# Attention and gated FFN in one kernel: the third batch's first queries and keys move ahead of the last weights in the load list, and three hand-kept orders of work are replaced

## The chip, the core and the metric

The kernel runs on one core of a Trainium2 chip. The metric is the device time of one execution in microseconds (us). The core has TensorE (PE: matmuls, with PEld for its weight loads), VectorE (DVE), ScalarE (ACT), GpSimd (POOL) and SyncE (SP). POOL issues all loads from memory, SP issues the DMA transposes and most stores, ACT a few stores at the end.

## What is computed

The reference, cut to its core:

```python
# q, k, v: (8 batches, 12 heads, 448 positions, 64)
scores = scale * np.matmul(q, k.transpose(0, 1, 3, 2))
attn = np.maximum(scores, 0.0) ** 2 / S
attn_out = np.matmul(attn, v)
x = attn_out.transpose(0, 2, 1, 3).reshape(B * S, H * D)   # (3584, 768)
g = x @ w_gate                                             # (768, 1536)
out = (0.5 * g * (1.0 + erf(g / sqrt(2))) * (x @ w_val)) @ w_out
```

Attention with a squared relu in the place of softmax, and on its result a feed-forward block with a gelu gate. Inputs and output are float32; the kernel casts to bf16 while loading.

## The kernel before

**Work on TensorE.** The array is used as four quarters of 64 x 64; two row halves run as two streams of instructions, PE0 and PE1, and every matmul goes through the helper `mm` (line 400, its call of the matmul is line 401, where nearly all of PE's rows stand). Per batch there are:

- 21 score units ("s", `add_scores`): four matmuls of 64x64x448 each, then a relu on ACT (twice on DVE, in the first batch) and a square on DVE.
- 6 value products ("v", `add_values`): 14 matmuls, one for each pair of heads; their scaled result, copied by DVE or ACT, is one sixth of the batch's x (`xT`).
- gate and value sums of the FFN. A plain unit (`add_gate_value`) is 24 matmuls for one block of 128 of the 1536 columns, gate or value; batches 0 and 1 have 24 plain units each. Later batches also have units of seven products that share sums (`add_pair`, three-character names such as 2A1, 12 matmuls each).
- output products (`add_product`, names a1 to n7: 14 groups of seven products, 24 matmuls of 64x64x384 each), with weight sums made once on DVE (`add_weight_sums`, line 1139, `wt<-wo`).

A plain unit of a batch needs all six of that batch's value products, and the weights of its block: the weight tile W_i (gate half `wg`, value half `wv`) covers the blocks 2i and 2i + 1.

**Transposes of queries and keys.** A third of a batch (four heads) is called (b, m), with m from 0 to 2. For batches 0 and 1 PE transposes them ("t"). From batch 2 on, DVE regroups a third (`qkr`, line 511), and SP issues two DMA transposes of it (line 516, `add_dma_transposes`), which give `qkT`.

**The orders.** Three strings carry them.

- `START` (line 36) lists PE's first work, batch 0: transposes t00 to t21, score units s0 to s20, value products v0 to v5, single matmul pairs x0 and x1 of the first gate and value unit, and t30, batch 1's first transposes. An "a" behind a name puts that entry's copy on ACT in the place of DVE.
- `LINE` (line 12) lists all later units, 563 entries: a single digit is the next plain unit of that batch in the order of blocks, gate then value; "s" and "v" are the next score unit and value product of batches 1 to 7, "t" the next transposes of batch 1; the other names are as above, and "w0" to "w5" place weight sums on DVE.
- `LOADS` (line 33) lists the loads after batch 0's first ones. W is a gate and value weight tile, O a quarter of the output weights, "q" and "v" with a small letter are batch 0's; Qn and Vn are the queries with keys, and the values, of third n counted from batch 1: Q0 to Q2 are batch 1, Q3 and Q4 are the first two thirds of batch 2. What is in no list is loaded behind it, third by third.

**The planner.** `run_plan` (line 119) goes through these with a cost for each operation and writes each engine's program in the order of its own times. POOL's loads keep the list's order. For PE it looks at the first 12 units of `LINE` that are left (`AHEAD`, line 114; `next_unit`, line 168) and takes the first that it thinks ready, else the one that is ready soonest. The time at which it thinks a load landed comes from a sum over the loads alone:

```python
        arrivals[op] = nbytes / rate                 # load, line 432
            dma = max(dma, op.end) + arrivals[op]    # run_plan, lines 289, 290
            op.lag = dma + 2.0 - op.end
```

The programs that come out are fixed: on the chip each engine runs its own in order and waits on semaphores.

**Rings.** Queries and keys as loaded (`qk16`) have two buffers (`RING_H`), so Q_n waits for the transposes or the regrouping of the third two before it; values have three (`RING_V`), each freed by the third's last value product; `qkT` has three (`RING_T`). These waits stand on POOL's queue, in order, and hold up what is issued behind them.

**Fillers.** While PE waits in the first 24 us of the plan, `fill` puts in matmuls on a tile of zeros (`warm`, line 603).

Of the kernel before, what the change touches and what calls it, by code (L numbers as in the profile page):

```python
# [9 lines left out]


LINE = """
s s s 0 0 s t s 0 s s v 0 s s s s t s v 0 0 0 v 0 s s s s s v s v 0 s s 0 s v 0 1 0 0 1 1 1 1 s 1 0
0 1 0 s s 1 0 s s s 1 s 1 1 w1 v s s 1 1 s 0 1 1 1 0 s 1 s s 0 1 0 s s 0 1 v 1 1 1 1 a1 s a2 s s s
a7 a6 1 v a4 s a5 v s b7 s b1 s b6 v w0 a3 s s b5 b4 b2 s v 2 s b3 s 2 s 2 s 2 v 2 s 2 s s s s v s
s s v 2 s 2 2 c1 c6 v c7 s s v 2 c2 c4 2 c5 s s 2 v s s 2A1 2D1 s 2A7 2D7 w2 2A2 2A6 c3 s s s 3 2D6
2A5 2A4 v 2D2 2D4 s 3 v 2D5 2F1 s 2E1 2F2 2A3 3 s 2F6 s 2D3 2E7 2F7 s 2E6 v 2E2 2E5 2E4 2E3 3 s 2C1
2F5 s 3 2C6 2F4 2B1 2C2 v 2C7 2B6 2B7 2C5 s s s 2F3 2B5 s 2C4 s 3 2C3 w3 s s s 2B2 s 2B4 3 2B3 3 d1
d7 d6 3 3 v v s s e1 s s e2 d5 e7 d4 d3 v d2 s s s e6 v s f7 3 s 3 s f1 e4 f6 s s f5 e5 s s 4 f4 4
v s s f3 v f2 4 4 v s s e3 s s 4 4 4 s s s g7 v 4A1 s g1 s s s s v v g6 4 5 s 4A7 4A2 4A6 g5 g2 g4  # L20
4D1 4A4 s s 4E1 4A5 4E2 v s 4A3 4D7 g3 4D6 4E6 s 4D5 4D2 5 4E7 4E4 s 4B1 4E5 s s 4F1 s 4B6 v 4D4
4D3 s s 4B7 v 4B2 4G1 4B5 4B4 s 4F6 4F7 4F2 4G6 4E3 4B3 4G2 s 4H1 s 4F5 4F4 4F3 4G7 v 4C1 s s 4H2
4H7 4G5 4H6 4G4 s 4H4 4H5 s 4G3 s 4C6 s v v 4C7 4C5 4C2 5 4C4 s s 4C3 s 5 5 h7 4H3 h1 s 5 5 s h6 s
h5 i1 5 i7 s i6 s v s s s h3 v i4 h2 6B1 h4 v 6A1 s s v 6B2 i5 i3 6A6 6A2 j1 j7 j2 i2 6A7 6B7 6D1
6G1 6A4 6B6 j6 j4 6A5 6B4 w4 6D7 j5 6D6 6B5 6G6 6G7 6A3 6D2 w5 6G5 j3 6G2 6C1 6C2 6B3 6C6 6D4 6E1
6D5 6E2 6C7 6H1 6G4 6C5 6C4 6E7 6D3 6G3 6E6 6H2 6L1 6H7 6E5 6H6 6H4 6K1 6H5 6C3 6L2 6K2 6L6 6E4 6K6
6L7 6L5 6H3 6K7 6F1 6I1 6E3 6F6 6F7 6J1 6F2 6K5 6K4 6F5 6L4 6I2 6I6 6F4 6J6 6I7 6L3 6J2 6J7 6K3 6F3
6I5 6I4 6J5 k7 6J4 6I3 6J3 l1 n1 l6 k1 k6 k5 k4 k3 l7 l4 m7 m1 m2 n7 n2 m6 l5 l3 n6 m4 m5 n5 n4 l2
# [12 lines left out]

# [266 lines left out]
def kernel(  # L308
# [162 lines left out]
    def load_v(b, h0, h1, deps=()):  # L471

        m = h0 // 4
        for i in range(2):
            def emit(i=i):
                if (b, m) not in v16:
                    v16[b, m] = qkv.tile([128, 4, VC, D], bf16, name="v16", tag="v16")
                c0 = i * (SC - VC)
                return nc.gpsimd.dma_start(  # L479
                    v16[b, m][HALF[i], h0 % 4:h0 % 4 + h1 - h0, :, :],  # L480
                    v[b, h0:h1].rearrange("h (p c) d -> p h c d", c=SC)[:, :, c0:c0 + VC, :])
# [1121 lines left out]
```

## Time and profile before

| What | us |
|---|---|
| runs shown: median (lowest, highest of 3) | 394.53 (394.39, 396.39) |
| the profiled execution, first to last instruction | 397.0 |
| PE busy in it | 388.1 |
| first matmul on loaded data starts at | 5.68 |
| first score unit of batch 2 starts at | 83.22 |
| last store issued by ACT at | 392.88 |

The profiled execution is an execution of its own, 2.5 us above the median; all times of the trace below are its times, counted from its first instruction. In the rows, "x" is a count of instructions, "out<-in" names tiles, and a bracket at the end of a row gives how long the engine had been idle and what released it. Loads are counted in KB as they land (bf16), half of what is read.

### The profile page before, as it was taken

What the parts mean: (1) busy time and instruction counts of PE and PEld (TensorE: products, weight loads), DVE (VectorE), ACT (ScalarE), POOL (GpSimd) and SP (SyncE); (2) the same over time, 40 slices, a digit from 0 to 9 for tenths busy, and PEclk for the clock granted to TensorE, in tenths of its full rate; (3) what the DMA queues carried; (4) which work ended last, traced back from release to release, by engine and by line L of the source; (5) the groups of instructions that cost most, each with busy time, mean ns of one, the idle gap of its engine ahead of it and who ended that gap; (6) DMA issues with size and microseconds to landing.
All of it is one profiled execution on the core that took longest, in us unless ns stands there. A gap on an engine that the chain in (4) does not pass through costs nothing.

```text
span 397.0 us, 18156 instructions
## 1 busy us (share of the span) xinstructions
PE 388.1 (98%) x8195; PEld 335.3 (84%) x8198; DVE 297.5 (75%) x479; ACT 268.5 (68%) x428; POOL 95.7 (24%) x156
## 2 busy tenths in 40 slices
PE   7999999999999999999999999999999999999995
PEld 3355689978988998899999989889999998899994
DVE  2695795767797688889878669698999577778652
ACT  2795872266687778988577787889877656665320
POOL 5755523322233333123123333130100000000000
PEclk9999999999999999999999999999999999999999
DMA  7999999998989999856588998964302240000055
GB/s 91 168 200 198 197 207 201 93 117 105 122 152 152 199 110 179 107 73 97 71 138 144 140 200 123 146 94 56 50 2 62 64 122 2 4 3 2 23 142 160
DMA packets 76333, 44.82 MB, mean 113 GB/s; under 512 B 36832, under 2 KB 73184, under 8 KB 76256
## 3 DMA queue, kind: packets, MB, share of 16 engines
q0 software_dynamic: 37728, 24.39, 47.7%
q1 hardware_dynamic: 37888, 18.49, 26.4%
q8 instruction: 64, 1.05, 1.1%
q10 hardware_dynamic: 640, 0.79, 0.7%
q14 instruction: 13, 0.11, 0.1%
HBM read 48.76 MB, written 11.01 MB: 151 GB/s over the span
## 4 chain that ended last, share of the span: by engine, by line
PE 81%; DMA 15%; POOL 1%; issue 1%; ACT 1%; DVE 0%; SPq 0%; ACTq 0%; POOLq 0%; DVEq 0%
PE ff L401 71%; PE sp L401 8%; DMA qk<-in_k_dram 5%; DMA wg<-in_moe_w_gate_dram 3%; DMA wv<-in_moe_w_val_dram 3%; DMA qkT<-qkr 2%; PE ff L603 1%; DMA v<-in_v_dram 1%; DMA out_dram<-osb 1%; PE ff L683 1%; POOL v L479 0%; POOL wg L440 0%; SPq L516 0%; PE ff L645 0%; ACT attnT L751 0%
## 5 line engine op out<-in xcount | busy, mean ns | idle before, releaser
L401 PE MATMUL ff<-xT,wg 64*64 64x448 bf16 x1680 | 179.8, 349 | 0.4 <-ACT xT L841 0.4
L751 ACT ACTIVATE attnT<-sp 128x896 bf16<-128x896 f32 x148 | 134.0, 921 | 31.0 <-PE sp L401 30.4
L401 PE MATMUL ff<-xT,wv 64*64 64x448 bf16 x1056 | 114.4, 349 | 0.0
L401 PEld LDWEIGHTS <-wg 64*64 64x64 bf16 x1680 | 101.2, 107 | 9.7 <-issue 0.9
L401 PEld LDWEIGHTS <-wv 64*64 64x64 bf16 x1680 | 101.5, 107 | 9.0
L770 DVE TENSOR_TENSOR attnT<-attnT 128x1792 bf16<-128x1792 bf16 (+1 forms) x84 | 82.1, 987 | 15.0 <-ACT attnT L751 14.8
L401 PEld LDWEIGHTS <-s 64*64 64x64 bf16 x1344 | 77.8, 107 | 4.6 <-issue 0.4
L401 PE MATMUL sp<-qkT 64*64 64x448 bf16 x672 | 78.3, 358 | 1.2 <-DMA qkT<-qkr 0.4
L401 PE MATMUL ff<-attnT,v 64*64 64x448 bf16 x600 | 74.0, 350 | 0.2 <-DVE attnT L770 0.2
L401 PE MATMUL ff<-xT,ws 64*64 64x448 bf16 x624 | 71.1, 349 | 0.0
L401 PE MATMUL ff<-ts,wv 64*64 64x448 bf16 x624 | 68.8, 349 | 0.0
L401 PE MATMUL ff<-wo,s 64*64 64x384 bf16 x672 | 62.4, 323 | 0.0
L401 PE MATMUL ff<-wt,s 64*64 64x384 bf16 x672 | 60.9, 323 | 0.0
L401 PEld LDWEIGHTS <-ws 64*64 64x64 bf16 x936 | 56.0, 107 | 3.9
L1011 DVE TENSOR_TENSOR part<-ff,part 128x448 f32<-128x448 f32 x78 | 47.4, 622 | 15.4 <-PE ff L401 11.1
L401 PEld LDWEIGHTS <-uT 64*64 64x64 bf16 x912 | 55.8, 107 | 2.7
L401 PE MATMUL ff<-wo,uT 64*64 64x384 bf16 x576 | 55.3, 322 | 0.0
L460 POOL DMA_DIRECT2D qk<-in_q_dram x43 | 26.6, 620 | 96.7 <-ACT attnT L751 76.4
L401 PEld LDWEIGHTS <-v 64*64 64x64 bf16 x672 | 40.7, 107 | 6.0 <-issue 1.3
L1007 ACT COPY part<-ff 128x448 f32<-128x448 f32 x78 | 40.2, 539 | 7.9 <-PE ff L401 6.1
L1319 ACT COPY osb<-ff 128x384 f32<-128x384 f32 x56 | 26.6, 482 | 28.0 <-PE ff L401 22.5
L1109 DVE TENSOR_TENSOR uT<-gel,ff 128x448 bf16<-128x448 bf16 x44 | 27.2, 620 | 20.7 <-PE ff L401 18.0
(69 smaller groups left out, 471.4 us busy)
## 6 DMA issues: line engine op xcount, KB each, us to landing
out_dram<-osb SPq DMA_DIRECT2D x48, 192.0 KB, 3.7
v<-in_v_dram POOLq DMA_DIRECT2D x48, 128.0 KB, 5.3
qk<-in_q_dram POOLq DMA_DIRECT2D x38, 112.0 KB, 3.9
qk<-in_k_dram POOLq DMA_DIRECT2D x38, 112.0 KB, 4.2
wg<-in_moe_w_gate_dram POOLq DMA_DIRECT2D x6, 384.0 KB, 9.5
wv<-in_moe_w_val_dram POOLq DMA_DIRECT2D x6, 384.0 KB, 10.9
wo<-in_moe_w_out_dram POOLq DMA_DIRECT2D x4, 576.0 KB, 14.7
qk<-in_q_dram POOLq DMA_DIRECT2D x5, 224.0 KB, 7.0
```

Source lines behind the costliest of these rows:

```text
L401: ins = nc.tensor.matmul(o, lhsT, rhs, start=start, stop=stop, skip_group_check=onto, tile_position=(P * row, P * col))
L460: return nc.gpsimd.dma_start(qk16[b, m][HALF[i], g0 - 4 * m:g1 - 4 * m, :], src[b, g0:g1].rearrange("h (p c) d -> p h (c d)", c=SC))
L603: blocks.add(nc.tensor.matmul(t[:, 0:cols], warm[:, 0:128], warm[:, 0:cols], start=True, stop=True))
L683: blocks.add(nc.tensor.transpose(t[HALF[j], c, :], src[:, 2 * r + j, c, :], ident[:, :], tile_position=(0, P * j)))
L751: relu.ins = nc.scalar.activation(o, x, AF.Relu).ins
L770: nc.vector.tensor_tensor(a[:, part], a[:, part], a[:, part], op=ALU.mult)
L1007: rd.ins = nc.scalar.copy(st["t", name][:, :], box[0][:, 0:S]).ins
L1011: rd.ins = nc.vector.tensor_tensor(t[:, :], box[0][:, 0:S], t[:, :], op=ALU.add).ins
L1109: u_op[b, fc].ins = nc.vector.tensor_tensor(uT[b][:, fc, :], gel.pop((b, fc))[:, :], box[0][:, 0:S], op=ALU.mult).ins
L1319: ins = nc.scalar.copy(o, box[0][:, 0:OGS])
```

## The change

`LOADS` gets a new order, in which Q3 and Q4 stand ahead of the last weight tiles; `START` and `LINE` get new orders of the same entries, except that in `START` "v3a" becomes "v3" and "v5" becomes "v5a". The load behind the lists skips values that are loaded already. A second way of adding up a pair's first two products is added under `TRICK`, which is 0, so its branches (in `add_pair`, left out here but for the switch) are not taken. No other constant changes.

```diff
 LINE = """
-s s s 0 0 s t s 0 s s v 0 s s s s t s v 0 0 0 v 0 s s s s s v s v 0 s s 0 s v 0 1 0 0 1 1 1 1 s 1 0
-0 1 0 s s 1 0 s s s 1 s 1 1 w1 v s s 1 1 s 0 1 1 1 0 s 1 s s 0 1 0 s s 0 1 v 1 1 1 1 a1 s a2 s s s
-a7 a6 1 v a4 s a5 v s b7 s b1 s b6 v w0 a3 s s b5 b4 b2 s v 2 s b3 s 2 s 2 s 2 v 2 s 2 s s s s v s
...
-m3 n3 k2
+0 0 0 s s 0 s t s s 0 s 0 0 v s s s s s 0 0 t s v s s 0 0 0 s s s 0 v s s 0 0 0 v s v s s v 0 s 0 1
+0 s 1 s 0 s 1 s 1 1 0 s v s 1 1 1 1 1 s s 1 s s 1 s 0 1 v s s 1 1 1 s s 1 1 1 s 1 s v w1 s 1 1 v a1
+s a6 1 s 1 s a7 b1 v v b6 b7 b2 a5 b4 2 s a2 a4 s v s 2 2 s s a3 s b5 s s s v b3 2 2 s s v 2 s s 2 s
...
+6I4 6I3 m1 k7 6J3 l7 k6 k5 m2 l1 m7 l6 l5 k4 k3 m6 l3 n1 n6 n7 n4 m5 l4 n5 m3 l2 n3 n2 k2 m4
 """
-LOADS = "q8 v4 v8 W0 Q0 W1 Q1 V0 W2 V1 Q2 W3 V2 W4 W5 O0 O1 O2 O3"
+LOADS = "q8 v4 v8 W0 Q0 Q1 V0 W1 V1 W2 Q2 Q3 V2 O0 W3 W5 Q4 W4 O2 O3 O1"
 START = """
-t00a s0 s1 t01 s2 s3 s4 s5 s6 t10 s7 t11 s8 s9 s10 t20 t21 s11 v0 s12 s13 v1 s14 v2a s15 s16 x0 v3a
-s17 x0 s18 x1 x1 x1 s19 v4a s20 f x0 x0 x0 x1 v5 t30
+t00a s0 s1 t01 s2 s3 s4 s5 t10 s6 s7 s8 t11 v1 s9 s10 t20 s11 v0 s12 t21 s13 v2a s14 s15 s16 x0 x0
+s17 s18 x1 v3 s19 x0 v4a s20 x1 x1 f x0 x1 x0 v5a t30
 """
...
+    TRICK = 0
...
-            load_v(b_, 4 * m_, 4 * m_ + 4)
+            if (b_, m_) not in v_loads:
+                load_v(b_, 4 * m_, 4 * m_ + 4)
```

More of the change, by code (lines that the diff above doesn't have):

```diff
@@ L18 @@
[L18 to L28, printed above, removed]
@@ L29 @@
-m3 n3 k2
+0 0 0 s s 0 s t s s 0 s 0 0 v s s s s s 0 0 t s v s s 0 0 0 s s s 0 v s s 0 0 0 v s v s s v 0 s 0 1
+0 s 1 s 0 s 1 s 1 1 0 s v s 1 1 1 1 1 s s 1 s s 1 s 0 1 v s s 1 1 1 s s 1 1 1 s 1 s v w1 s 1 1 v a1
+s a6 1 s 1 s a7 b1 v v b6 b7 b2 a5 b4 2 s a2 a4 s v s 2 2 s s a3 s b5 s s s v b3 2 2 s s v 2 s s 2 s
+2 2 c1 s s v s c2 2 s s v 2 c6 s c7 2 v s 3 s 2A1 w0 2D1 s s 2A7 2A2 c5 2D7 s 2D6 2A6 s c4 2D2 2D5 s
+2D4 s c3 w2 s 3 2A4 2A5 2F1 2A3 3 s 2F6 v 2E1 2F2 3 2F7 v 2D3 2E7 s s 2F4 s 2E6 3 2C1 v 2E5 2F5 2E2
@@ new lines @@
+3 2C7 2F3 2E4 s 2C6 2E3 2B1 2C5 s 2C2 v s 2B6 2C4 s 3 s 2B2 2B7 2B4 s 2B5 v d1 2C3 s s 2B3 3 s s s s
+d2 s s 3 s v 3 s s d6 d7 v d4 3 3 4 e7 d5 e1 e6 s d3 s f1 s v e2 f6 e4 f7 s v v f4 f5 s s f2 s 4 s
+e5 v s 4 s 4 s 4 s s e3 f3 s v 4 s s 4 4A1 s s 4 g1 v s v 4A2 g6 g7 s 4A7 s g5 g3 g2 4E1 4A6 s 4D1
+g4 4A4 4E6 4E2 4D2 4E7 5 s 4D6 4A5 4D7 4D4 4E5 w3 s 4E4 4D5 4A3 4D3 s 5 4B1 v 4B6 4B2 4B7 s v 4F1
+4F2 4B5 4B4 4E3 4B3 s 4H1 4F6 4G1 4F7 s s s 4G2 s 4F4 s 4F5 4G6 s 4H2 s v s 4G7 4F3 4H6 v 4H7 s 4G5
@@ new lines @@
+4C1 4H4 4C2 4G4 s 4C7 s 4H5 s 4C6 4G3 4H3 4C4 v 4C5 s 4C3 s 5 h1 s h2 5 h7 v s h6 5 5 h4 w4 s h5 5 s
+5 v i1 s i7 i6 i2 s s v i4 h3 s i5 s 6B1 s i3 6A1 j7 s j1 s v j2 v 6B6 6B2 6A2 j6 6B7 6B4 6A7 j4 6D1
+j5 6B5 6A6 6G1 6D2 6D7 w5 6A4 j3 6B3 6A5 6G7 6G6 6G2 6D6 6D5 6E1 6A3 6G5 6C1 6E2 6E7 6C2 6E6 6E5 6H1
+6C7 6H2 6G4 6D4 6K1 6D3 6H7 6L1 6G3 6H6 6H5 6C6 6K2 6E4 6L6 6K7 6H4 6C4 6E3 6L7 6L2 6C5 6F1 6J1 6C3
+6F7 6L5 6K6 6F6 6L4 6F2 6K4 6H3 6I1 6K5 6F5 6J2 6L3 6I6 6J7 6K3 6J6 6F4 6F3 6I7 6I5 6I2 6J4 6J5 k1
@@ L349 @@
     GATE_T, BLOCK = 0, 7.1
-    NPB = (0,0,3,3,4,4,6,6)
+    NPB = 0, 0, 3, 3, 4, 4, 6, 6
     TWO = 2, 4, 6
@@ L963, in add_pair @@
         stage = stages[name]
-        if name in opens:
+        onto = TRICK and name == "2"
+        opening = name in opens and not onto
+        if opening:
             st["box", stage] = {}
@@ L967, in add_pair @@
         else:
-            free = [st["read", stage]]
+            free = [st["read", "1" if onto else stage]]
+        if TRICK and name == "1":
+            st["box", "Z"] = {}
         box = st["box", stage]
@@ L986, in emit @@
                 wait_lower(box)
+            if TRICK and name == "1" and r == 0 and k == 0:
+                z = st["box", "Z"]
+                z[0] = new_bank(z["k"], st["read", "1"])
+                if "cover" in z:
+                    for j in range(2):
+                        mm(z[0][HALF[j], OGS:S], warm[HALF[0], HALF[j]], warm[HALF[0], 0:S - OGS], 0, j, True, True)
             mov = ts[b, x][:, :, :] if isinstance(x, int) else xT[x[0]][:, x[1], x[2]]
@@ L992, in emit @@
                          a()[HALF[r], c, o + P * j:o + P * (j + 1)], mov[HALF[r], c, :], r, j,
-                         name in opens and r == 0 and k == 0, r == 1 and c == K3 - 1, True)
+                         opening and r == 0 and k == 0, r == 1 and c == K3 - 1, True)
             box[1] = ins
@@ L1003, in add_pair, with emit_onto @@
             reads_x.setdefault(x[0], []).append(last)
+        def emit_onto():
+            rd.ins = nc.scalar.copy(st["box", "Z"][0][:, 0:S], box[0][:, 0:S]).ins
         def emit_copy():
@@ L1043, in mult @@
             return m
-        if name in "167":
+        if TRICK and name == "1":
+            rd = Op("ACT", 0.5, emit_onto, [last], lag=0.2, prio=0)
+            ACT.append(rd)
+        elif onto:
+            rd = gelu(lambda: box[0][:, 0:S], [last], 0.06)
+        elif name in "167":
             rd = Op("ACT", 0.5, emit_copy, [last], lag=0.2, prio=0)
@@ L1064, in add_pair @@
             mult("3", "7", b1, c1, st["sum", "5"], st["half"])
-        then(at, GS, *ops, box if name in opens else None, lambda: st["read", stages_last[stage]])
+        then(at, GS, *ops, box if opening else None, lambda: st["read", stages_last[stage]],
+             (st["box", "Z"], lambda: st["read", "2"]) if TRICK and name == "1" else None)
     opened = {}
```

2 lines of the change are left out of this document (removed).

## The prediction

> **What bounds the kernel now.** The page's busy table and slices come first, then the table by stage (each row: stretch, its length, then each engine's busy time with its count, granted clock, DMA share, GB/s).
>
> ```profile
> PE 388.1 (98%) x8195; PEld 335.3 (84%) x8198; DVE 297.5 (75%) x479; ACT 268.5 (68%) x428; POOL 95.7 (24%) x156
> PE   7999999999999999999999999999999999999995
> ```
>
> ```profile
> 0.00:5.70 5.70, 3.64 (x18) 1.33 (x19) 0.28 (x2) 1.49 (x2) 4.58 (x13) 1.00 0.53 61
> 5.70:15.00 9.30, 9.00 (x69) 3.61 (x70) 5.01 (x7) 4.73 (x6) 6.24 (x10) 1.00 1.06 146
> 15.00:32.00 17.00, 15.65 (x246) 8.55 (x246) 13.64 (x23) 13.64 (x18) 8.44 (x13) 1.00 1.38 193
> 32.00:40.00 8.00, 8.00 (x170) 4.88 (x168) 5.16 (x8) 5.44 (x8) 5.54 (x8) 1.00 1.40 198
> 82.00:84.00 2.00, 1.56 (x33) 0.93 (x27) 1.26 (x3) 0.35 (x1) 0.00 (x0) 1.00 1.22 130
> 84.00:392.00 308.00, 308.00 (x6792) 280.06 (x6784) 242.04 (x393) 220.21 (x362) 56.42 (x92) 1.00 0.64 97
> 392.00:397.00 5.00, 0.23 (x4) 0.00 (x0) 0.00 (x0) 0.48 (x1) 0.00 (x0) 0.92 0.61 177
> ```
>
> TensorE is the bound, at a granted clock of 1.00. Busy time flatters it, since a quarter of the array counts as all of it, so count matmuls. Between 55 and 82, the same table for line 401 alone says:
>
> ```profile
> 55.00:82.00 27.00, 27.00 (x579) 25.80 (x572) 1.00 1.09 153
> ```
>
> That is 27 us / 579 = 46.6 ns for each 64x64x448 matmul at full use. By this price 15 to 32, with x246 (short transposes and fillers among them), is well short of the 365 that would fit, 82 to 84 has 33 of 43, and from 84 to 392 PE is never idle. So there are three places where an order can win: the start up to about 34 us, the hole at 83, and small half-empty spells. The change does not touch the number of matmuls: both orders hold the same 563 entries, so the price of the work itself is unchanged.
>
> **The hole at 83.** The chain that ended last, in order of time (start, length, what), then PE and its weight load in the timeline:
>
> ```profile
> 26.10 11.59 DMA wv<-in_moe_w_val_dram
> ...
> 40.22 12.14 DMA wg<-in_moe_w_gate_dram
> 52.64 14.71 DMA qk<-in_k_dram
> 67.43 3.76 DMA v<-in_v_dram
> 71.19 0.75 DVE wt L1152
> 72.58 1.32 SPq L516
> 73.94 9.23 DMA qkT<-qkr
> ```
>
> ```profile
> 83.22 0.14 PEld L401 LDWEIGHTS <-qkT 64*64 64x64 bf16 x7 [0.87 <-issue]
> ```
>
> ```profile
> 83.22 0.38 PE L401 MATMUL sp<-qkT 64*64 64x448 bf16 x4 [0.44 <-DMA qkT<-qkr]
> ```
>
> Batch 2's first keys land at 52.64 + 14.71 = 67.35, behind all weights; regrouping and two DMA transposes end at 73.94 + 9.23 = 83.17, and the first score unit of batch 2 starts 0.05 us later. PE is idle 0.44 us and without new weights 0.87; I take 0.8 as the loss (33 against 43 matmuls gives 0.47, with some counted from before 82).
>
> **The loads, step by step.** Sizes (KB as landed) and rate:
>
> ```profile
> v<-in_v_dram POOLq DMA_DIRECT2D x48, 128.0 KB, 5.3
> wg<-in_moe_w_gate_dram POOLq DMA_DIRECT2D x6, 384.0 KB, 9.5
> wo<-in_moe_w_out_dram POOLq DMA_DIRECT2D x4, 576.0 KB, 14.7
> qk<-in_q_dram POOLq DMA_DIRECT2D x5, 224.0 KB, 7.0
> ```
>
> From the landing of W2's value half (26.10 + 11.59 = 37.69) to W5's gate half (40.22 + 12.14 = 52.36) came V1, Q2, W3, V2, W4 and half of W5: 256 + 448 + 768 + 256 + 768 + 384 = 2880 KB in 14.67 us, 196 KB/us. So Q costs 2.3 us of the stream, V 1.3, a W 3.9, an O 2.9. In the new order W2 has V1 ahead as well: 39.0. Then Q2 41.3, **Q3 43.6** (before: 67.35 and after), V2 44.9, O0 47.8, W3 51.7, W5 55.7, Q4 57.9, W4 61.9, O2 64.8, O3 67.7, O1 70.7. Before, by the same prices, W3 ended at 45.2 and W4 at 50.4; W1, at 37.69 - 3.9 - 1.3 - 2.3 = 30.2, moves to 33.8. Thus W1 is 3.6 us later, W3 6.5, W4 11.5, W5 about 1.4.
>
> With Q3 in at 43.6, one regrouping copy (0.63) and the transposes at the measured 9.23 give keys by about 56 at the latest. Where does PE ask for them? Behind the start list stand, in the new order, entries worth 27.1 us before the 22nd "s" (30.0 before the change), priced 1.12 us for a gate or value unit (24 x 46.6 ns), 0.19 a score unit, 0.65 a value product, 0.97 a "t" (row below). The start ends with the transposes "t30":
>
> ```profile
> 31.40 0.97 PE L683 MATMUL sp<-ident,qk 128*64 128x128 bf16 x28
> ```
>
> 32.4 + 27.1 = 59.5, after 56. So the hole goes: **-0.8 us**. What is late next is V(2,0), which POOL issues only after O1 (about 72, as now), and the values that need it; PE has other units then.
>
> What the step moves along: Q3 and Q4 are eight issues on POOL, 0.7 us each by the rows below, and each group waits for the qk ring of two buffers. Q3 waits for the transposes of batch 1's second group, at list place 8 (5.1 us of work, 37.5 us), 4 us ahead of its turn in the stream. Q1 now stands before W1 and V0 and waits for "t21", which START puts after s12 instead of before s11:
>
> ```profile
> 20.52 0.68 POOL L460 DMA_DIRECT2D qk<-in_q_dram  x1
> 21.14 0.67 POOL L460 DMA_DIRECT2D qk<-in_k_dram  x1
> 23.81 1.23 POOL L479 DMA_DIRECT2D v<-in_v_dram  x2 [2.01 <-PE sp L401]
> ```
>
> Two score units more, at ACT's pace of 0.92 (a row in the next part), move Q1's issue to about 22.4 and W1's, formerly ahead of it, to about 25. The stream then still holds W0 and Q0 to about 26 (30.2 less W1's 3.9), so I cost the wait at nothing; without that cover, 1 us later is 1 us of W1. V0's 2.01 us wait for a value product goes, since "v1" moves ahead of s9. On SP the two transposes are first in line.
>
> **The start.** ACT and DVE carry it: 19 of 21 first-batch scores go through ACT.
>
> ```profile
> 8.20:29.30 21.10, 19.92 (x251) 9.73 (x257) 16.79 (x28) 17.34 (x21) 13.02 (x19) 1.00 1.30 182
> ```
>
> ```profile
> 16.89 0.92 ACT L751 ACTIVATE attnT<-sp 128x896 bf16<-128x896 f32 x1 [0.70 <-PE sp L401]
> ...
> 26.99 0.56 ACT L841 ACTIVATE xT<-ff 128x448 bf16<-128x448 f32 x1
> ```
>
> ACT idles 21.10 - 17.34 = 3.76 us and DVE 4.31. The 0.70 at 16.89 waits for s7, which waits for the transposes t10, which stand behind s6; the new START puts t10 before s6, so I take 0.7. The copy at 26.99 is "v3a", ahead of the last two ACTIVATEs; as "v3" it goes to DVE, and the last one, "v5a", comes to ACT. Of its 0.56 I take 0.3, because DVE has squares queued there. Sum **-1.0 us**, bounds +0.56 (the copy only delays DVE by its own length) and -3.76 (all ACT idle time goes).
>
> **The rest of the order.** From 84 on only half-empty spells are left, such as
>
> ```profile
> 117.77 0.10 PEld L401 LDWEIGHTS <-s 64*64 64x64 bf16 x1 [0.43 <-issue]
> ```
>
> A reordering removes some and makes others; I take **-0.3**, with bounds of three such rows either way, -1.3 and +1.3. The tail (392.37 copy, store, 397.0) ends with a product's read and a store in both orders: 0.
>
> ```profile
> 392.37 0.48 ACT L1319 COPY osb<-ff 128x384 f32<-128x384 f32 x1 [0.60 <-PE ff L401]
> ```
>
> Sum: -0.8 - 1.0 - 0.3 = -2.1 us, 397.0 to 394.9 for the profiled execution. That execution is 2.5 us over the median of the runs (394.53); I carry the difference along: **392.4 us**, 0.53% less.
>
> **Are the weights covered?** This is where the sum can break. Without W3, W4 and W5 PE has after 32.4: 10 units of W0 to W2 (11.2 us), two "t" (1.9), 21 score units (3.9), 6 value products (3.9): 20.9 us, to 53.3. Batch 1's own units cannot begin before its six value products are done, place 46 and 27.3 us in, near 59.7. W3's gate half lands at 49.8, its value half at 51.7: 3.5 us of cover, and in the list W3's first unit stands 17.1 us in, at 49.5. Before, it stood 21.0 us in, at 53.4, with W3 landed at 45.2: 8 us of cover. The change spends most of it.
>
> **Rivals.**
> *Transposes in the load stream (slower).* The two DMA transposes of batch 2 used to run when the stream was done; now they start near 46 with O0, W3 and W5 queued. Loads alone, loads with transposes, and the regrouped tile:
>
> ```profile
> 50.00:70.00 20.00, 20.00 (x429) 17.92 (x425) 14.72 (x24) 10.65 (x16) 5.38 (x9) 1.00 1.23 203
> 74.00:84.00 10.00, 9.56 (x201) 8.74 (x196) 5.09 (x10) 2.45 (x5) 2.62 (x5) 1.00 1.28 119
> ```
>
> ```profile
> 83.29 0.63 DVE L511 COPY qkr<-qk 128x1792 bf16<-128x1792 bf16 x1 [0.73 <-DMA qkT<-qkr]
> ```
>
> 128 x 1792 bf16 are 459 KB, 46 GB/s over those 10 us, so loads got about 73 of 203: 6.4 us of stream lost. W3 would land at 56 and 58, past the 53.3. It decides from a delay of 3.5 us. The planner books arrivals of loads alone (`arrivals` in `load`), so PE's order, and DVE's in-order weight sums behind O1, would wait: up to 6.4 on top of 392.4, **398.8**. Against it: 70 to 84 also held few loads at first, and in the view of who waited for whom no weight load ends a PE wait now. The Trainium skill, "DMA: Bandwidth & Descriptors", section "Issuing engines are not separate DMA queues", says that DMAs started by different engines run on the same 16 DMA engines and interleave; the trace agrees (203 against 119 GB/s), and the rule speaks for this rival.
> *The start gives up all of ACT's idle time.* -0.8 - 2.8 - 0.9 = -4.5: **390.0**. For it: t10, t21 and v1 all move where PE had fillers; against: DVE is as full.
> *Nothing net.* The score hole goes, but a like one opens where W1 or W3 is late; or PE was only relieved of waits that its other units share. **394.5**. For it: 98% busy.
>
> **Chances.** Forecast 0.48 (own range 390.4 to 394.2), transposes 0.25, whole start 0.13, nothing net 0.14. A measurement of this kernel can tell about 0.5%, 2.0 us: below 392.56 or above 396.5. Of the forecast 0.26 lies below 392.56, so faster is 0.26 + 0.13 = 0.39; same 0.22 + 0.14 + 0.03 = 0.39; slower 0.22. Range 389.8 to 398.8: it leaves out the start's far bound (0.06) and a second delay, Q4's transposes ahead of O1 (0.12).
>
> **What would show it.** Right: batch 2's first score starts before 62 without a wait on qkT; no 0.7 idle of ACT near 16; PE at 43 matmuls in each 2 us from about 33 on. Wrong: PE waiting on wg or wv between 45 and 65, GB/s under 130 there, DVE waiting on wo near 70 to 85. If weights wait, the third step (cover) failed; if the start is no shorter, the second.

## The result, and the profile after

| | median us (lowest to highest) | ratio to before, 95% interval |
|---|---|---|
| before | 394.8 (394.39 to 396.39) | |
| after | 405.01 (402.76 to 407.21) | 1.0244 [1.0201, 1.0288] |

The change makes the kernel 2.4% slower, and the prediction (392.4 us, at most 398.8) was wrong. The profiled execution of after took 402.76 us by the clock of the runs and 401.0 us from its first instruction to its last. Its page, busy time and slices:

```profile
PE 386.8 (96%) x8198; PEld 340.2 (85%) x8198; DVE 292.6 (73%) x472; ACT 271.9 (68%) x435; POOL 95.2 (24%) x156
...
PE   8999959979999999999999999999999999999994
...
PEclk9999998999999999999999999999999999999999
```

TensorE is still the bound, but it now has two dents, in the slices around 55 and 83, and a slice with less clock between them. Which waits make them is in the table of what PE waited for (total us, times, longest):

```profile
PE sp L401 <- DMA qkT<-qkr: 5.7, 2, 3.5
...
PE ff L401 <- issue: 1.1, 2, 0.6
```

Both long waits are for `qkT`, the transposed keys of batch 2. The chain of work that ended last holds three DMA transposes (start, length):

```profile
45.86 13.35 DMA qkT<-qkr
65.52 12.67 DMA qkT<-qkr
78.21 5.38 DMA qkT<-qkr
```

So the second transpose of third (2,0) ran from 45.86 to 59.21, and PE's first score unit of batch 2 started at 59.35; the second transpose of (2,1) ended at 83.59, and PE's next wait ended there. In the timeline the two ends and the pace behind the first one (start, length; the bracket gives the idle time):

```profile
59.35 0.59 PE L401 MATMUL sp<-qkT 64*64 64x448 bf16 x4 [3.46 <-DMA qkT<-qkr]
...
60.07 0.61 PE L401 MATMUL ff<-xT,wg 64*64 64x448 bf16 x2
...
60.44 0.61 PE L401 MATMUL ff<-xT,wg 64*64 64x448 bf16 x2
...
83.63 0.57 PE L401 MATMUL sp<-qkT 64*64 64x448 bf16 x8 [2.25 <-DMA qkT<-qkr]
```

Pairs of matmuls on both halves stand 0.37 us apart behind the wait, twice the normal distance (0.19 again from 62.85 on). The table by stage gives the reason, the granted clock of 0.51:

```profile
55.50:59.30 3.80, 0.39 (x11) 0.00 (x0) 0.99 (x1) 0.41 (x1) 0.70 (x2) 0.99 1.33 190
59.30:62.70 3.40, 3.35 (x40) 1.96 (x44) 1.16 (x2) 1.39 (x3) 2.75 (x5) 0.51 1.44 199
62.70:66.00 3.30, 3.30 (x76) 2.08 (x72) 2.16 (x3) 3.28 (x6) 1.24 (x2) 1.00 1.19 210
```

Forty matmuls in 3.4 us, where 76 ran in the next 3.3. In busy time this stretch looks full (3.35 of 3.40): only the count and the clock show it.

**Where the time went.** The profile of before that the prediction used turned out to be an odd one (below, e5). Against a second profile of the unchanged kernel, with a span of 392.9 us, the same table by stage reads, the second profile of before first:

```profile
40.00:84.00 44.00, 43.98 (x934) 32.13 (x930) 32.11 (x50) 22.73 (x35) 15.06 (x25) 1.00 1.22 169
84.00:340.00 256.00, 256.00 (x5616) 231.19 (x5608) 206.03 (x326) 195.49 (x315) 54.65 (x89) 1.00 0.69 106
```

```profile
40.00:84.00 44.00, 37.24 (x738) 25.82 (x732) 28.14 (x41) 24.32 (x37) 17.64 (x27) 0.96 1.33 185
84.00:340.00 256.00, 255.94 (x5641) 244.73 (x5634) 199.89 (x317) 192.90 (x311) 52.12 (x86) 1.00 0.67 103
```

Between 40 and 84 after does 196 matmuls fewer; at the prediction's 46.6 ns that is 9.1 us. From 84 to 340 it does 25 more, 1.2 us back. Together 7.9 us, against a difference of the spans of 401.0 - 392.9 = 8.1. **In these two executions the whole loss lies between 40 and 84.** Its parts, as far as rows name them: 3.5 and 2.2 us of waiting for `qkT`, 1.7 us at half clock (3.4 us at 0.51), and a remainder of about 1.7 us in shorter spells, the two "issue" waits of 1.1 us among them.

The medians differ by 10.2 us, some 2 us more than these two executions. The profiled one was the fastest of after's four, and the four times rise as the mean granted clock falls (402.76 us at 0.995, 404.97 at 0.994, 405.05 at 0.992, 407.21 at 0.990). That fits more time at half clock in the others; no profile of them was kept.

### The profile page after: what moved, and what is told of

It is laid out like the page before. It is cut to its first block, busy times and chain, and to the rows that moved or that the text cites. A ratio compares the mean times of both kernels' runs of the same rounds, so it can differ in the third digit from the quotient of the medians.

```text
span 401.0 us, 18154 instructions
## 1 busy us (share of the span) xinstructions
PE 386.8 (96%) x8198; PEld 340.2 (85%) x8198; DVE 292.6 (73%) x472; ACT 271.9 (68%) x435; POOL 95.2 (24%) x156
## 4 chain that ended last, share of the span: by engine, by line
PE 86%; DMA 10%; DVE 1%; issue 1%; ACT 1%; SPq 0%; ACTq 0%; POOL 0%; POOLq 0%
PE ff L401 76%; PE sp L401 8%; DMA qkT<-qkr 8%; DMA out_dram<-osb 1%; DMA qk<-in_k_dram 1%; PE ff L603 1%; PE sp L683 1%; DVE uT L770 1%; PE ff L683 1%; DVE qkT L687 0%; DVE attnT L749 0%; ACT attnT L751 0%; SPq L516 0%; PE ff L645 0%; DVE osb L1336 0%
## 5 line engine op out<-in xcount | busy, mean ns | idle before, releaser
L401 PE MATMUL ff<-xT,wv 64*64 64x448 bf16 x1056 | 112.4, 350 | 1.1 <-issue 1.1
L401 PEld LDWEIGHTS <-wv 64*64 64x64 bf16 x1680 | 102.8, 107 | 9.6 <-issue 2.3
L401 PEld LDWEIGHTS <-wg 64*64 64x64 bf16 x1680 | 102.3, 107 | 8.9 <-issue 1.4
L401 PEld LDWEIGHTS <-s 64*64 64x64 bf16 x1344 | 78.9, 107 | 3.4 <-issue 0.6
L401 PE MATMUL ff<-attnT,v 64*64 64x448 bf16 x600 | 76.9, 352 | 0.1
L401 PE MATMUL ff<-ts,wv 64*64 64x448 bf16 x624 | 71.6, 349 | 0.0
L401 PEld LDWEIGHTS <-ws 64*64 64x64 bf16 x936 | 57.3, 107 | 3.3
L401 PE MATMUL ff<-wt,s 64*64 64x384 bf16 x672 | 58.9, 323 | 0.1
L401 PE MATMUL ff<-wo,uT 64*64 64x384 bf16 x576 | 52.3, 323 | 0.0
L401 PEld LDWEIGHTS <-v 64*64 64x64 bf16 x672 | 42.9, 108 | 4.0 <-issue 1.1
```

Of the source, the lines that this page charges most:

```text
L401: ins = nc.tensor.matmul(o, lhsT, rhs, start=start, stop=stop, skip_group_check=onto, tile_position=(P * row, P * col))
```

## The experiments

Three questions: which of the three lists costs the time; why the keys come late; and what of the prediction's start and clock holds. Times are medians with the lowest and highest of the runs; the kernel before, run beside them, had medians of 395.49 to 395.75 us.

### Which list

**e5**, the kernel before, unchanged: what an undisturbed profile of it looks like.

> The kernel before once more, for a second profile of it. In the first one the granted clock is on record only from 13.9 us, in all later profiles of these kernels from 3.9 to 5.3 us. If that execution was a slow starter: the clock stands from about 5 us, the span is about 393 instead of 397, PE has by 35 us as much done as the changed kernel, and one short wait on qkT stands near 79 to 80. If START made the difference: span 397 again and the first plain unit at 34 us.

Measured 395.75 (394.5 to 397.97), ratio 1.0003 [0.9982, 1.0025]. In this profile batch 2's first score stands at 78.93 with no wait on `qkT` on the list: the hole at 83, on which the prediction put 0.8 us, is not there in it. And its first 15 us differ from those of the first profile. Rows of the first profile's timeline:

```profile
9.77 0.59 PE L401 MATMUL sp<-qkT 64*64 64x448 bf16 x4
...
13.98 0.38 PE L401 MATMUL sp<-qkT 64*64 64x448 bf16 x4
```

The same four matmuls take 0.59 us before 13.9 us and 0.38 behind it: that execution ran at about half clock for its first 14 us (in after the same four take 0.59 us where 0.51 is on record). The clock of 1.00 in the prediction's rows there was a blank, not a reading: the clock record of that profile begins at 13.9 us, in the other profiles at 3.9 to 7.2 us. In e5 the score unit at 7.66 already takes 0.38. The start stage, e5 and after, one fence each:

```profile
5.70:15.00 9.30, 9.00 (x106) 3.88 (x104) 7.52 (x13) 7.46 (x10) 7.62 (x12) 1.00 1.25 174
15.00:32.00 17.00, 16.16 (x272) 9.07 (x276) 12.53 (x21) 12.81 (x17) 8.90 (x14) 1.00 1.40 198
```

```profile
5.70:15.00 9.30, 8.84 (x105) 3.86 (x104) 7.21 (x12) 7.37 (x9) 6.80 (x11) 1.00 1.22 170
15.00:32.00 17.00, 16.71 (x272) 9.06 (x270) 12.95 (x22) 13.10 (x17) 9.10 (x14) 1.00 1.40 198
```

106 and 272 matmuls before, 105 and 272 after: the new start gains nothing that the counts show. The wait of 0.70 us of ACT that it was to remove is in e5 as well, and after has one of 0.74 in its place, one unit earlier; the last copy then waits longer, 1.31 us where e5 has 0.62. ACT, e5 and after:

```profile
13.03 0.92 ACT L751 ACTIVATE attnT<-sp 128x896 bf16<-128x896 f32 x1 [0.70 <-PE sp L401]
```

```profile
12.41 0.92 ACT L751 ACTIVATE attnT<-sp 128x896 bf16<-128x896 f32 x1 [0.74 <-PE sp L401]
...
27.62 0.54 ACT L841 ACTIVATE xT<-ff 128x448 bf16<-128x448 f32 x1 [1.31 <-PE ff L401]
```

**e3**, before with the new load list alone:

```diff
-LOADS = "q8 v4 v8 W0 Q0 W1 Q1 V0 W2 V1 Q2 W3 V2 W4 W5 O0 O1 O2 O3"
+LOADS = "q8 v4 v8 W0 Q0 Q1 V0 W1 V1 W2 Q2 Q3 V2 O0 W3 W5 Q4 W4 O2 O3 O1"
```

> The kernel before with the new load list alone. Theory A: DMA transposes of batch 2's first third are issued before 55 us with loads on the way, take 10 us or more, and PE waits 2 us or more on qkT: 398 to 404. Theory B: PE waits on weights, 398 to 404 too, but the wait stands on wg or wv and not on qkT. Theory C: no change, 393 to 396.

Measured 411.52 (410.77 to 413.87), ratio 1.0403 [1.0367, 1.0439]: more than either theory said. Its waits of PE:

```profile
PE sp L401 <- DMA qkT<-qkr: 8.2, 2, 4.4
...
PE ff L401 <- DMA wv<-in_moe_w_val_dram: 0.5, 1, 0.5
```

The loads alone bring the late keys, as the change itself does. That is not all of it: against e5 this run does 242 matmuls fewer between 40 and 84 (692), 11.3 us by 46.6 ns, and 116 fewer from 84 to 340 (5500), 5.4 us.

**e4**, before with the new start alone:

```diff
-t00a s0 s1 t01 s2 s3 s4 s5 s6 t10 s7 t11 s8 s9 s10 t20 t21 s11 v0 s12 s13 v1 s14 v2a s15 s16 x0 v3a
+t00a s0 s1 t01 s2 s3 s4 s5 t10 s6 s7 s8 t11 v1 s9 s10 t20 s11 v0 s12 t21 s13 v2a s14 s15 s16 x0 x0
...
```

> The kernel before with the new START alone. The trace of the changed kernel has done, by 34 us, about 4 us more of PE's work than that of before. If START alone does it: 390 to 391.5. If it takes the new loads or LINE as well (theory C2): 393 or more.

Measured 398.85 (398.49 to 399.11), ratio 1.0072 [1.0054, 1.009]: 0.7% slower, not 4 us faster. The loss does not lie in the start: from 40 to 84 this run does 930 matmuls where e5 does 934, from 84 to 340 5538 where e5 does 5616. That expectation still took the slow beginning of the first profile for something that a better order could win.

**e2**, after with the old load list, and **e11**, before with the new order of later units alone:

```diff
-LOADS = "q8 v4 v8 W0 Q0 Q1 V0 W1 V1 W2 Q2 Q3 V2 O0 W3 W5 Q4 W4 O2 O3 O1"
+LOADS = "q8 v4 v8 W0 Q0 W1 Q1 V0 W2 V1 Q2 W3 V2 W4 W5 O0 O1 O2 O3"
```

> The changed kernel's START and LINE with the load list of before, so batch 2's transposes run when the weights are in. Theory A: the two holes at 55 to 63 and 81 to 84 go, one like that of before (0.8 us at 83) may come back, the 4 us gained before 35 us stay: 390 to 393. Theory B: the same sign, since the weights are early again, 390 to 393; this run tells both from theory C (the new LINE itself asks for things in a bad order, whatever the loads): 398 or more.

```diff
 LINE = """
-s s s 0 0 s t s 0 s s v 0 s s s s t s v 0 0 0 v 0 s s s s s v s v 0 s s 0 s v 0 1 0 0 1 1 1 1 s 1 0
+0 0 0 s s 0 s t s s 0 s 0 0 v s s s s s 0 0 t s v s s 0 0 0 s s s 0 v s s 0 0 0 v s v s s v 0 s 0 1
...
```

> The kernel before with the new order of later units alone; load list and start as before. Theory C: old loads and new units gave 403.8 with the new start, and the new start alone 398.9; if the two costs add up the time is 399 to 401, with a wait on qkT near 80. If the units' order is neutral by itself, 394 to 396.

Measured: e2 403.83 (399.62 to 404.67), ratio 1.0171 [1.0106, 1.0236]; e11 403.9 (401.77 to 406.32), ratio 1.0213 [1.0167, 1.026]. In e2 theories A and B (390 to 393) both fell and theory C was met; e11 is above both of its ranges. With the old loads the keys come at 80, and the new order asks for them at 78. The stages around that point, e2 first:

```profile
78.10:79.85 1.75, 0.38 (x5) 0.00 (x0) 0.00 (x0) 0.54 (x1) 0.00 (x0) 1.00 1.70 168
79.85:83.40 3.55, 3.55 (x34) 2.52 (x37) 1.72 (x2) 2.14 (x3) 1.19 (x2) 0.58 0.83 48
83.40:87.20 3.80, 3.80 (x45) 3.26 (x41) 1.58 (x2) 1.90 (x3) 1.18 (x2) 0.50 0.97 155
```

```profile
78.10:80.30 2.20, 0.39 (x5) 0.00 (x0) 0.00 (x0) 0.54 (x1) 0.00 (x0) 1.00 1.66 167
80.30:83.70 3.40, 3.38 (x32) 2.39 (x35) 1.72 (x2) 2.03 (x3) 1.19 (x2) 0.59 0.78 61
```

A wait of 1.4 us in e2 is followed by 6.8 us at about half clock, which is 3.4 us lost, and one of 1.8 us in e11 by 3.4, which is 1.7 us lost. The rest of their loss lies behind 84: 5526 and 5527 matmuls from 84 to 340, where e5 has 5616.

**e12**, after with the old order of later units, and **e15**, after with the old start, close the table; the edits are those of e11 and e4 the other way round:

```diff
 LINE = """
-0 0 0 s s 0 s t s s 0 s 0 0 v s s s s s 0 0 t s v s s 0 0 0 s s s 0 v s s 0 0 0 v s v s s v 0 s 0 1
+s s s 0 0 s t s 0 s s v 0 s s s s t s v 0 0 0 v 0 s s s s s v s v 0 s s 0 s v 0 1 0 0 1 1 1 1 s 1 0
...
```

> The changed kernel with the old order of later units; load list and start are new. The new load list with old start and old units gave 411.5. Theory A with theory C: the old order asks for batch 2's keys at the place that suits their old landing, but the plan reorders within 12 units and takes the early arrivals at their word, so waits on qkT of 5 to 9 us and 408 to 414. If the new start is what fits the new load list, 400 to 404.

```diff
 START = """
-t00a s0 s1 t01 s2 s3 s4 s5 t10 s6 s7 s8 t11 v1 s9 s10 t20 s11 v0 s12 t21 s13 v2a s14 s15 s16 x0 x0
+t00a s0 s1 t01 s2 s3 s4 s5 s6 t10 s7 t11 s8 s9 s10 t20 t21 s11 v0 s12 s13 v1 s14 v2a s15 s16 x0 v3a
...
```

> The changed kernel with the old start list; load list and later units are new. The new start cost 3 us with old loads and old units (398.9 against 395.7) and nothing with the other pairs (403.8 against 403.9, 413.2 against 411.5). If it is neutral beside the new lists, 404 to 406; if it costs here too, 401 to 403.

Measured: e12 413.17 (411.81 to 414.06), ratio 1.0453 [1.0425, 1.0482]; e15 405.34 (404.13 to 407.32), ratio 1.0252 [1.0213, 1.029]. e12 waits 8.5 us in all for `qkT`, as forecast; in e15 the new start is neutral. All eight combinations, in us:

| later units | old loads, old start | old loads, new start | new loads, old start | new loads, new start |
|---|---|---|---|---|
| old | 395.75 (e5) | 398.85 (e4) | 411.52 (e3) | 413.17 (e12) |
| new | 403.9 (e11) | 403.83 (e2) | 405.34 (e15) | 405.01 (after) |

The parts do not add up. The new loads cost 14 to 16 us beside the old order of units and about 1 us beside the new one; the new order of units costs 5 to 8 us beside the old loads and saves 6 to 8 beside the new ones. The new start costs 3 us, 1.7 us or nothing. Each list fits the times of the others, so "the part that costs" isn't to be had by taking one list back. The kernel before is the best of the eight.

### Why the keys are late

**e9** and **e10**, after with its own lists, and only the moved loads put back to the end: both (Q3, Q4), and Q4 alone.

```diff
-LOADS = "q8 v4 v8 W0 Q0 Q1 V0 W1 V1 W2 Q2 Q3 V2 O0 W3 W5 Q4 W4 O2 O3 O1"
+LOADS = "q8 v4 v8 W0 Q0 Q1 V0 W1 V1 W2 Q2 V2 O0 W3 W5 W4 O2 O3 O1 Q3 Q4"
```

> The changed kernel with its own start and order of units, its own order of weights, output weights and values; only the two groups of queries and keys of the third batch (Q3, Q4) go back to the end of the load list. If the transposes in the load stream are all that the change cost (theory A), no wait on qkT is left between 50 and 66 and the time is 395 to 399. If the new orders cost by themselves, because each list fits only the times of the others (theory C), the wait moves to where the keys now land (near 80) and the time stays at 402 to 407, as with the old load list.

```diff
-LOADS = "q8 v4 v8 W0 Q0 Q1 V0 W1 V1 W2 Q2 Q3 V2 O0 W3 W5 Q4 W4 O2 O3 O1"
+LOADS = "q8 v4 v8 W0 Q0 Q1 V0 W1 V1 W2 Q2 Q3 V2 O0 W3 W5 W4 O2 O3 O1 Q4"
```

> The changed kernel with Q4 alone at the end of the load list; Q3 stays ahead. Theory A, with the first wait as the larger part: the wait on qkT near 59 stays at 2 to 4 us, the weights behind it (W4, O1) land some 2 us earlier, the time is 402 to 405. If Q4's loads and transposes are what disturbs (the rival), the wait near 59 goes below 1 us and the time is 396 to 400.

Measured: e9 401.81 (399.5 to 404.27), ratio 1.016 [1.011, 1.0209]; e10 416.5 (414.91 to 417.49), ratio 1.0526 [1.0495, 1.0558]. PE's waits for keys, e9 and then e10:

```profile
PE sp L401 <- DMA qkT<-qkr: 0.7, 1, 0.7
```

```profile
PE sp L401 <- DMA qkT<-qkr: 3.1, 2, 2.8
```

In e9 the wait near 59 is gone, as theory A has it, and one of 0.7 us stands at 78.5, where the keys now land, as theory C has it. The time lies between the two theories' ranges: the stage from 40 to 84 is nearly whole (890 matmuls), but from 84 to 340 it does 5563, 78 fewer than after. In e10 the wait near 59 stays (2.8 us), so the rival there fell; its time is far above both ranges, because its later order came out worse too (728 matmuls from 340 to 380, where after has 894).

**e1**, after, with the planner told that these transposes take 13 us in the place of 5:

```diff
-                          [copy], lag=5.0) for i, (c0, c1) in enumerate(((0, VC), (VC, SC)))]
+                          [copy], lag=13.0 if (b, m) in ((2, 0), (2, 1)) else 5.0) for i, (c0, c1) in enumerate(((0, VC), (VC, SC)))]
```

> The changed kernel with one number altered: the planner books 13 us in the place of 5 for the landing of the DMA transposes of batch 2's first two thirds. Loads and all three lists stay. Theory A (the transposes share the DMA engines with the loads and take 13 us, while the order of PE's units was made for 5): PE gets other units in those places, the waits of 3.46 and 2.25 us on qkT go, and the time falls from about 403 to 405 to 392 to 396. Theory B (the weights that now come later starve PE; the transposes only happen to be what it waits for last): PE waits on wg or wv in the same stretch, and the time stays above 400.

Measured 418.92 (418.56 to 422.84), ratio 1.0602 [1.0552, 1.0653]. No wait on `qkT` is left; in its place stand

```profile
PE ff L401 <- DMA wg<-in_moe_w_gate_dram: 2.6, 2, 1.9
PE ff L401 <- DMA wv<-in_moe_w_val_dram: 1.9, 1, 1.9
...
PE ff L401 <- DMA v<-in_v_dram: 0.9, 1, 0.9
```

With batch 2's scores put off, PE stands before W3 (0.7 and 1.9 us) and W4 (1.9 us). In part it uses up the weights sooner, in part they come later: W3's value half landed at 54.03 here, at 50.00 in after. That is the prediction's first rival (weights late), seen once the keys are taken out of the way. By the words of its expectation this run speaks for theory B (waits on wg and wv, above 400). It does not decide, since the units' order changed with it: more than half of the loss lies behind 84 (5438 matmuls from 84 to 340, 721 from 340 to 380), where the plan had fallen into another order. e7 and e16 below decide.

**e7**, after, with the output weights O0 and every load listed behind them held until both transposes of (2,0) are done:

```diff
+            tr_op[b, m][i].ins = ins.ins
...
+    wo_op[0].behind += tr_op[2, 0]
+    wo_op[0].deps += tr_op[2, 0]
```

> The changed kernel, but the load O0 and all behind it wait until the two DMA transposes of batch 2's first third have landed. Theory A (the transposes are slow because loads share the engines): the pair lands within 7 us of its issue (13 to 15 in the changed kernel), the first score unit of batch 2 waits for nothing, and as the stream pauses for those us PE waits on W3 or W5 (wg, wv) instead, 2 to 6 us; time 398 to 408. Rival D (a pair of transposes in flight takes 10 us by itself): it lands after 10 us or more although no load is on the way, and PE waits on both.

Measured 405.61 (404.06 to 405.99), ratio 1.0235 [1.0208, 1.0262]. The two transposes' median time from issue to landing, after and e7 (table of DMA issues):

```profile
qkT<-qkr SPq DMA_TRANSPOSE x2, 11.9
```

```profile
qkT<-qkr SPq DMA_TRANSPOSE x2, 4.5
```

10.4 and 13.4 us beside the loads, 4.1 and 5.0 without them: **the loads make the transposes slow.** The Trainium skill, "DMA: Bandwidth & Descriptors", section "Issuing engines are not separate DMA queues", says that DMAs started by different engines run on the same 16 DMA engines and interleave; e7 agrees with its numbers. The row of 9.23 us that the prediction used lies between: in its time 0.67 MB were loaded, 73 GB/s. In after, the stage of the two transposes was

```profile
44.46:59.21 14.75, 10.87 (x223) 9.25 (x212) 8.00 (x10) 10.07 (x15) 4.24 (x7) 1.00 1.41 175
```

The transposes' 459 KB are 31 GB/s of that and the loads' 2.07 MB are 140, against the 198 of the stage from 15 to 32: both are slowed. Nothing was won by the hold, since the weights behind it came 8 to 12 us later (W3's value half at 61.58 in the place of 50.00, W5's at 66.39 in the place of 58.39). PE's longest waits in e7:

```profile
PE sp L401 <- DMA qkT<-qkr: 3.2, 1, 3.2
PE ff L401 <- DVE uT L1129: 1.4, 2, 1.2
```

The 3.2 us are the transposes of (2,1), which the hold did not cover; one ran behind the other, 13.8 and 6.4 us from issue to landing. The first score unit of batch 2 waited for nothing, as theory A has it, but the wait of 2 to 6 us on weights that it forecast was only 0.6 us (`wv`): most of e7's loss is in stages where PE is counted busy with fewer matmuls (810 from 40 to 84).

**e13** and **e14**, after with the first one or the first two thirds of batch 2 transposed by TensorE, like those of batches 0 and 1, so that no DMA transpose stands in for them:

```diff
-    FIRST_T = 6
+    FIRST_T = 8
...
-        if m and b == EARLY:
+        if (b, m - 1) in tr_op and b == EARLY:
...
-    flow_t = [(1, m, (0, 1)) for m in range(1, FIRST_T - NM)]
+    flow_t = [(t // NM, t % NM, (0, 1)) for t in range(NM + 1, FIRST_T)]
```

That is e14; e13 has `FIRST_T = 7`. In `LINE` a "t" is set in for each such third, five places ahead of its first score unit.

> The changed kernel with the first third of batch 2 transposed by TensorE (28 matmuls, 0.97 us a third in the profile of before, and one copy on DVE) in the place of a regrouping copy and two DMA transposes; the unit stands five places ahead of the first score unit that needs it. Theory A: the wait near 59 is the DMA transposes beside the loads; it goes with its clock stretch (3.5 us and about 1.7), TensorE pays 1 us, the loads behind Q3 land some 3 to 6 us earlier, the second wait near 83 (2.3 us) stays: 400 to 402. Rival: the keys are asked for too early in any case, because all loads together are late; then a wait for loads (wv, wg, v or k) of 2 us or more takes the place: 404 or more.

> The same for the first two thirds of batch 2: no DMA transposes run while the listed loads are under way, but Q4 lands only at about 60 in the stream, so its transposes by TensorE come at once behind it. Theory A: both waits go, TensorE pays 2 us: 397 to 400. Rival: 403 or more, with waits for loads.

Measured: e13 414.75 (413.29 to 415.7), ratio 1.0482 [1.0448, 1.0515]; e14 407.86 (407.33 to 408.02), ratio 1.0312 [1.0285, 1.0339]. Both miss theory A's times and lie in the rivals' ranges, but without the waits for loads of 2 us or more that the rivals go by (0.5 us in e13). By stage, e14 does what it says up to 84:

```profile
40.00:84.00 44.00, 44.00 (x941) 36.08 (x937) 34.67 (x51) 27.87 (x41) 19.78 (x30) 1.00 1.28 185
84.00:340.00 256.00, 256.00 (x5545) 235.44 (x5539) 197.00 (x313) 190.31 (x309) 50.35 (x83) 1.00 0.68 100
340.00:380.00 40.00, 39.14 (x734) 29.98 (x730) 25.61 (x45) 17.70 (x37) 0.00 (x0) 1.00 0.01 3
```

941 matmuls where after has 738 and before 934 (56 of the 941 are the added short ones of the two thirds). Its longest wait for a load or for keys is the first row, and it stands in the start, at 7.4 us; e13's is the second:

```profile
PE ff L668 <- DMA qk<-in_k_dram: 0.6, 1, 0.6
```

```profile
PE sp L386 <- DMA qkT<-qkr: 3.8, 1, 3.8
```

What e14 won it lost behind 84: 96 matmuls fewer than after from 84 to 340, 160 fewer from 340 to 380. No transpose of these two thirds runs in those stretches; what differs there is the order in which the plan placed the units, after it had been given two more. e13's long wait is for the DMA transposes of (2,1), and it has the same late disorder (739 matmuls from 340 to 380).

**e16** takes the plan out of the comparison: e14 once more, with the units held to the order in which after's plan had placed them, the two "t" set in, and the plan free to look at only 2 units in the place of 12.

```diff
-AHEAD = 12
+AHEAD = 2
...
+    ORDER = [int(x) for x in '''
+        1 4 5 2 7 8 9 3 6 10 12 11 16 13 17 18 14 19 15 20 21 23 24 22 26
...
+    rank = {float(x): n for n, x in enumerate(ORDER)}
+    for u in later:
+        u.at = rank[u.at]
```

> The kernel of e14 (the first two thirds of batch 2 transposed by TensorE, no DMA transposes beside the listed loads), with the later units held to the order in which the changed kernel's plan had them, the two added units set in, and the plan allowed to look at 2 units in the place of 12. e14 lost nothing more than 1.9 us between 35 and 100 us but some 14 us from 150 on, where its plan had fallen into another order; the changed kernel lost 10 us between 45 and 90 and almost nothing behind. Theory A with C: both losses are gone, TensorE pays 2 us: 394 to 397, no slower than the kernel before. Rival (the late losses come from the added units themselves or from later loads): 402 to 408.

Measured 396.13 (395.39 to 396.36, 12 runs), ratio **1.0007 [0.9996, 1.0017]**. The loss of the change is gone. By stage:

```profile
40.00:84.00 44.00, 43.88 (x938) 31.00 (x932) 35.44 (x52) 26.98 (x40) 20.22 (x30) 1.00 1.26 186
84.00:340.00 256.00, 256.00 (x5629) 241.06 (x5625) 199.93 (x318) 193.22 (x314) 50.85 (x83) 1.00 0.69 100
340.00:380.00 40.00, 40.00 (x914) 34.81 (x910) 29.00 (x56) 19.63 (x39) 0.00 (x0) 1.00 0.11 28
```

What PE waited for holds one row for a load, at the very start, and none for keys:

```profile
PE ff L630 <- DMA qk<-in_k_dram: 0.2, 1, 0.2
```

No DMA transposes of (2,0) and (2,1) exist, and the first of (2,2) is issued at 75.64, when the listed loads have landed. W5's value half lands at 54.34 and W4's at 60.68, where after had 58.39 and 64.39: the transposes had cost the loads behind them about 4 us as well. Behind 84 its counts (5629 and 914) are near after's (5641 and 894), so the order was held. So with the new loads, the new start and (but for the two added units) the new order of units, what cost the time was the DMA transposes of batch 2's first two thirds beside the loads. e16 takes away the late keys, the half clock behind them and the delay of the loads all at once and doesn't price each; nor was after run with its order pinned and its DMA transposes kept. e16 pays 1.9 us of TensorE for it (two times the 0.97 us of such a third) and comes out level with before. It does not beat it; no kernel measured here does.

### Clock and start

**e6**, after, with 17 and 12 matmuls on zeros ahead of the first score units of (2,0) and (2,1), so that PE is busy while it would wait:

```diff
+                for _ in range({(2, 0): 17, (2, 7): 12}.get((b, u), 0)):
+                    nc.tensor.matmul(box[0][:, 0, :], warm[:, 0:128], warm[:, :], start=True, stop=True)
```

> The changed kernel with matmuls on zeros (17 and 12 of 128x512, some 3.6 and 2.6 us) put ahead of the first score units of batch 2's first and second third, where PE waits for keys. Theory A2 (an idle PE loses its clock: 0.51 granted from 59.3 to 62.7, so the hole of 3.46 us costs about 1.7 us more, and in the executions at 0.990 to 0.994 a multiple of that): no stretch at half clock between 40 and 95 us, score units still begin at 59 and 82 to 84, time 1.5 to 4 us under the changed kernel's 405, so 401 to 403.5, with a smaller spread. If the clock is no part of it: 404 to 407.

Measured 402.44 (401.86 to 407.27), ratio 1.0203 [1.0136, 1.0269], 2.6 us under after's median. The stretch behind the first wait:

```profile
59.30:62.70 3.40, 3.40 (x67) 1.92 (x68) 1.82 (x4) 2.34 (x4) 3.05 (x5) 1.00 1.43 195
```

Clock 1.00 in the place of 0.51, 67 matmuls in the place of 40; three of the 67 are the last on zeros, and the other 24 more are 1.1 us by 46.6 ns. The ranges of e6 and after overlap, and e6 has a wait of 1.3 us for values near 77 that after has not, so the 2.6 us are a rough size (the two profiled executions differ by 1.0 us); the row, not the median, shows that the clock was part of the loss.

**e8**, before with ten pairs of warm-up matmuls in the place of eight, to see whether a slow beginning such as the first profile's can be bought off:

```diff
-        for _ in range(8):
+        for _ in range(10):
```

> The kernel before with 20 instead of 16 matmuls on zeros at the very start, up to about 5.5 us, just short of the first keys at 5.6. If slow starts of the clock make up some of its spread (394.4 to 396.8): 0 to 1.5 us faster. If first matmuls on data are now behind the fillers: 0 to 0.5 us slower.

Measured 396.09 (395.23 to 397.49), ratio 1.0012 [0.9995, 1.0029]: nothing to win. Its profile (span 395.7) does show a wait of 1.2 us on `qkT` at 81, where the first profile of before has 0.44 and e5 none: the old order itself stands at the edge of this wait, and some of its executions go over it.

## Why the prediction was wrong, step by step

- **"keys by about 56 at the latest"** failed. The loads of Q3 came sooner than reckoned, the last at 41.44 where the sum has 43.6; DVE was busy with other work until 43.60 and started the regrouping copy then, so that the sum's start was right by luck. The failing term is the transposes "at the measured 9.23". That row was taken beside 73 GB/s of loads; beside 140 GB/s the same transpose took 13.35. By 9.23 the keys would have stood at 45.86 + 9.23 = 55.1.
- **"PE asks for them at 59.5"** failed. The working behind it was 32.4 for the end of the start list plus 27.1 us of list entries. 27.1 holds; 32.4 does not. The transposes that end the start list began at 31.40 in the profile used, and at 27.5 in e5 and in after, because the profiled execution had run at half clock until 13.9 us. The line's own view from 20 to 60 us (shortest, median, longest ns; first and last start), e5 and after:

```profile
L683 PE MATMUL sp<-ident,qk x84: 219/219/243, 27.5 to 41.9; 128*64 128x128 bf16 x84
```

```profile
L683 PE MATMUL sp<-ident,qk x84: 219/219/243, 27.5 to 42.8; 128*64 128x128 bf16 x84
```

59.5 less 3.9 is 55.6, and PE ran dry between 55.5 and 56. The transpose took 4.1 us more than in the sum, and the demand came 3.9 us sooner; by this arithmetic either error alone would just have left no wait, 59.2 against 59.5 or 55.1 against 55.6. Together they make the 3.5 us.
- **"So the hole goes: -0.8 us."** The hole at 83 of the first profile belongs to one execution at the edge; e5 has none. In after there is a longer one at the same place, 2.25 us, of (2,1): Q4's transposes, left in the prediction to a rival outside the range, took 12.67 and 5.38 us, and the kernel lets the second start only when the first has landed.
- **"Sum -1.0 us" for the start** failed: nothing, by the counts of e5 and after and by e15 against after; the new start alone (e4) even costs 3 us, behind 84. The wait at s7 from which 0.7 was taken is real, for e5 has it too, but the new order moved it and did not remove it: from 8.20 to 29.30 ACT idles 4.5 us in e5 and 4.4 in after.
- **"I carry the difference along"**, 2.5 us, misread the difference. In every later run the span is 1.7 to 1.9 us shorter than the time of the same execution by the clock of the runs, so a span of 397.0 stands for some 398.8, 4.2 us above the median. That was the slow beginning, not an offset of the kernel. The sum took no harm from it, since it comes to 2.1 us off the median either way; the times 31.40 and 83.22 did.
- **"I take -0.3"** for the rest of the order was right in sign and mis-sized: 25 matmuls from 84 to 340, -1.2 us, inside its bounds. The prediction gave no reason for the sign, and beside the old loads the new order loses there (e2, e11), so the sign was luck.
- **"3.5 us of cover" for the weights** held: after's list of PE's waits, down to 0.2 us, has none for weights, and W3 was there at 50.0, ahead of the 51.7 of the sum. It held narrowly: e6, with the same lists, waits 0.4 us for W3's value half near 52. Of the signs that the prediction named for being wrong, none showed; what showed was the wait on `qkT` that was not to be there.
- **The first rival** ("Transposes in the load stream") had the right place and the right cause, and e7 and e16 show it. Its victim was wrong: it had the loads slowed and PE waiting for W3, with "6.4 on top", 398.8. The loads were slowed, by 4.0 us at W5 and 3.7 at W4, but the transposes were slowed by as much, and PE came to the keys before it came to those weights. The weights become the victim when the keys are put off (e1, 4.5 us in all), and hardly when the keys are put first (e7, 0.6 us). Its price left out the clock (1.7 us) and the second third (2.2 us).

Open stays why the order that the plan falls into costs so much behind 84 when a list is changed alone (e3, e4, e11): e14 and e16 differ in that order and by 11.7 us, which shows its size, not its cause in each run. How the DMA engines share out between loads and transposes was not tried.

## What to carry to other kernels

Before a transfer is moved into a stretch where the transfers are the bound, price it from a row in which it ran beside such a load; when there is none, expect more than its worst row, as here the same transpose took 5.0 us alone, 9.2 beside 73 GB/s of loads and 13.4 beside 140. A planner that books one stream alone will place its users too early. Check that the profiled execution is an ordinary one before arguing from its beginning: the length of one known instruction form, early and late, tells the clock where the record is blank. Orders that fit each other's times are good only together, so test a part of a change with the rest of the order held fixed, as e16 did and e2 to e4 did not.
